# One fused attention and expert kernel on Trainium2: the chunk stage runs six tiles ahead instead of seven, with written lists for the prologue and for the last seven ticks

## The chip, the cores and the metric

One core of a Trainium2 chip. The metric is the device time of one execution in microseconds, the median of three runs. TensorE (PE in the profile) does matmuls and transposes; its weight loads are listed as PEld. VectorE (DVE), ScalarE (ACT) and GpSimd (POOL) work on tiles, and SyncE (SP) issues the transfers (DMA). Each engine works through its own queue in order and waits at the head of it for what an instruction needs. TensorE's clock has two levels, 1.2 and 2.4 GHz; the profile gives the granted clock as a share of the higher.

## The reference, cut to what matters

```
scores = scale * (q_c @ k_c^T)                # chunk attention: 64 rows, 8 heads, B = 8, S = 576
x = softmax(scores) @ v_c                     # 4608 rows x 512
logits = x @ w_gate                           # top 2 of 4 experts, softmax weights w
for e in range(4):
    a = softmax(causal(scale * (x @ wq[e]) @ (x @ wk[e])^T))
    out += mask_e * w_e * (a @ (x @ wv[e]) @ wo[e])
xn = layernorm(out) * g_ln
result = out + relu(xn @ w_ch1) @ w_ch2
```

## The kernel before, in words

The 4608 rows are 36 tiles of 128; nine tiles are a pair of batches, three tiles a group. A program of three kinds of work runs on them as a pipeline. The **chunk stage** of a tile takes q, k and v from memory: scores (`chunk_scores`, L145), shift by the row maximum (`chunk_shift`, L153, two VectorE instructions), exponential (`chunk_exp`, ScalarE), sum and reciprocal (`chunk_sum`, VectorE), scaling (`chunk_scale`, L171, GpSimd), turn (`chunk_turn`, L173: four transposes on TensorE and a copy on ScalarE), values (`chunk_values`, L181), and the split of the result x into a high part `xTh` (ScalarE) and the rest `xTl` (VectorE, `chunk_split`, L189), so that products keep more digits. The **projections** of a group (`proj_group`, L226) are seven pieces: four of `rows_` (k and q for two pairs of experts, 12 matmuls each) and three of `vals` (v and the gate's logits, one per tile). Each piece returns a copy for ScalarE and one for VectorE. The **attention** of a tile: scores (`attn_scores`, L328), masked shift (L376), exponential (L381), sums (`attn_sums`), weighing on GpSimd (`attn_weigh`, L398), transposes (`attn_turn`, L409), values (`attn_values`, L428), output projection (`attn_out`, L438) and the store to `xs`. A tile sees 1 to 5 key blocks of 128; at 5 it is "wide". When all is done, the second stage (normalising, two large matrix products, L838 and L1003) follows.

A **tick** s (`tick`, L557) does one step of each: the chunk stage of tile s, the chunk values of tile s-1, a few pieces of projections, and attention of tile g = s - `LA` (with transposes of g-1 and values and output of g-2). `LA` is 7: tiles 0 to 6 go through the chunk stage in a prologue. The order inside a tick is a string in `PLAN`, one letter per step, taken from left to right: S0 and S1 the scores of two pairs of experts, D0, D1, E0, E1 their masked shifts and exponentials, C chunk scores and values, H and X the split into xTh and xTl, N, n, R, r the chunk's shift, exponential, sum, scale, K and k its turn, O, Z, z attention values, Y, y output projection, L, W sums and weighing, T transposes, P or Q a piece of projections with a and v its two copies, G1 to G3 the gate, B one step of the conversion of the next stage's weights, F0, F1 (`fill`) one step of the preparation of the next stage. Four lists serve all ticks: by whether the tick is the third of a group, and wide.

The ticks 7 to 36 stand in a `manual_schedule`, in which TensorE, VectorE, ScalarE and GpSimd keep the order of the program. The prologue ahead of them and the ticks 37 to 44 don't: there a scheduler sets the order of each engine. SP's order is the scheduler's throughout.

The prologue's string `PRO` (L640) names loads of tiles (L), filler matmuls on zeros (`warm`, w), scores up to scale of a tile (S, five steps in one), turn with copy (P), values with split (X), a piece of the first group's projections with its copies (Q), and K, the next weights from `load_w` (L125). `load_w` loads a half of a weight into `wraw`, of which there are two buffers, and splits it into high (ScalarE) and low (VectorE) parts: wk, wq, wv, then wo, in this order. `pc`, the chunk probabilities, has two buffers as well.

## Time and profile before

| what | value |
|---|---|
| median of 3 runs | 1208.11 us (1207.94 to 1209.19) |
| the profiled execution | 1207.34 us, its span 1205.6 us |
| TensorE busy | 1179.7 us (98%) |
| VectorE, ScalarE, GpSimd busy | 902.2, 584.3, 266.6 us (75%, 48%, 22%) |
| mean granted clock of TensorE | 0.994 |

The span runs from the first to the last instruction; the execution's own time is 1.7 us longer. The attention of tile 0 begins at 49.28 us, and the second stage's first matmul at 466.03 us. TensorE is the engine that is nearly always busy, so that time is lost where it waits, runs at the lower clock, or does what the result doesn't need.

### The profile page before, as it was taken

The numbers are of one execution on the slowest core, as the hardware profiler recorded it, in microseconds if no ns is written. First come the engines' busy times: TensorE is split into PE (matmuls) and PEld (weight loads), VectorE is DVE, ScalarE is ACT, GpSimd is POOL, SyncE is SP. The second block draws the span as 40 slices with busy tenths as digits, with TensorE's granted clock in tenths as the row PEclk, the third lists the DMA queues.
The fourth block names the chain that finished last, engine by engine and source line by source line (L and its number), as shares of the span: only waits on it lengthen the run. The fifth ranks groups of instructions, "written<-read, shape, count | busy, mean of one in ns | idle before, by whom it ended". The sixth has DMA issues, their size and how long they took to land.

```text
span 1205.6 us, 29187 instructions
## 1 busy us (share of the span) xinstructions
PE 1179.7 (98%) x11874; PEld 1128.3 (94%) x11874; DVE 902.2 (75%) x1837; ACT 584.3 (48%) x1117; POOL 266.6 (22%) x480
## 2 busy tenths in 40 slices
PE   7989999999999999999999999999999999999998
PEld 5879998999999888999999999999999999999998
DVE  5688888888888768866865776556998777877782
ACT  3466566666566776533433343345454334333340
POOL 2245444644555331211121211110000000000000
PEclk8989999999999999999999999999999999999999
DMA  8333443434332236665455554658865445444521
GB/s 278 103 118 131 145 141 129 141 125 148 120 122 74 80 123 219 204 202 184 151 173 180 166 187 164 188 155 268 282 230 184 157 155 162 158 158 161 172 80 44
DMA packets 95845, 191.69 MB, mean 159 GB/s; under 512 B 8544, under 2 KB 42336, under 8 KB 94816
## 3 DMA queue, kind: packets, MB, share of 16 engines
q1 hardware_dynamic: 95712, 189.83, 47.4%
q8 instruction: 93, 1.52, 0.5%
q14 instruction: 40, 0.33, 0.1%
HBM read 118.50 MB, written 71.30 MB: 157 GB/s over the span
## 4 chain that ended last, share of the span: by engine, by line
PE 88%; DVE 6%; DMA 2%; ACT 1%; POOL 1%; issue 1%; SPq 0%; DVEq 0%; POOLq 0%; ACTq 0%
PE bb L838 17%; PE bb L1003 16%; PE ad L838 13%; PE ad L1003 12%; PE pp L246 7%; PE pv L273 4%; PE y_ps L438 4%; PE oa_ps L428 4%; PE tp L409 3%; PE sp L358 3%; PE tp L729 2%; PE sx_ps L151 1%; PE pT_ps L177 1%; DVE P L376 1%; PE sx_ps L187 1%
## 5 line engine op out<-in xcount | busy, mean ns | idle before, releaser
L838 PE MATMUL bb<-x,w1u 128*128 128x256 f32 x1728 | 216.6, 281 | 0.0
L838 PEld LDWEIGHTS bb<-x,w1u 128*128 128x128 f32 x1728 | 209.6, 188 | 0.3 <-ACT p L859 0.2
L838 PE MATMUL ad<-x,w1u 128*128 128x256 f32 x1296 | 173.3, 283 | 0.0
L838 PEld LDWEIGHTS ad<-x,w1u 128*128 128x128 f32 x1296 | 160.5, 188 | 0.2 <-issue 0.2
L1003 PE MATMUL bb<-w2u,hn 128*128 128x256 f32 x640 | 120.5, 280 | 1.5 <-DVE hn L951 1.5
L1003 PE MATMUL bb<-w2u,hx 128*128 128x256 f32 x584 | 109.5, 281 | 0.9 <-DVE xr L1014 0.9
L381 ACT ACTIVATE P<-P,nm 128x128 f32<-128x128 f32 (+8 forms) x144 | 87.2, 608 | 44.4 <-DVE nm L376 37.0
L398 POOL TENSOR_SCALAR P<-P,l 128x128 f32<-128x128 f32 (+8 forms) x144 | 94.5, 673 | 39.8 <-DVE l L391 24.8
L1003 PEld LDWEIGHTS bb<-w2u,hn 128*128 128x128 f32 x640 | 97.2, 189 | 1.7 <-DVE hn L951 1.7
L1003 PEld LDWEIGHTS bb<-w2u,hx 128*128 128x128 f32 x584 | 89.1, 189 | 1.0 <-PE bb L1003 1.0
L1003 PE MATMUL ad<-w2u,hn 128*128 128x256 f32 x440 | 80.7, 281 | 0.0
L1003 PE MATMUL ad<-w2u,hx 128*128 128x256 f32 x432 | 78.7, 281 | 0.0
L484 POOL TENSOR_TENSOR cv<-cv 128x512 f32<-128x512 f32 x16 | 25.5, 1594 | 235.8 <-DVE cv L480 218.3
L514 POOL TENSOR_TENSOR cw<-cw 128x128 f32<-128x128 f32 x128 | 62.3, 505 | 54.6 <-issue 46.4
L171 POOL TENSOR_TENSOR pc<-pc,lc 128x512 f32<-128x512 f32 x36 | 37.8, 1051 | 140.7 <-DVE lc L167 83.3
L1003 PEld LDWEIGHTS ad<-w2u,hn 128*128 128x128 f32 x440 | 65.7, 189 | 0.0
L1003 PEld LDWEIGHTS ad<-w2u,hx 128*128 128x128 f32 x432 | 64.9, 189 | 0.0
L376 DVE CUSTOM_DVE_ANT_0 P<-sp,mcaus 128x128 f32<-128x128 f32 (+7 forms) x128 | 59.9, 517 | 3.7 <-PE sp L358 3.6
L428 PE MATMUL oa_ps<-pTa,vg 128*64 128x128 f32 x928 | 59.4, 277 | 0.3 <-DVE pTa L413 0.3
L747 DVE TENSOR_TENSOR x<-xt,x 128x512 fp32r<-128x512 f32 x63 | 45.0, 722 | 19.2 <-ACT x L746 19.2
L409 PE MATMUL tp<-ident,P 128*128 128x128 f32 x464 | 57.9, 274 | 1.4 <-POOL P L398 1.3
L409 PEld LDWEIGHTS tp<-ident,P 128*128 128x128 f32 x464 | 52.0, 141 | 4.8 <-POOL P L398 1.8
(356 smaller groups left out, 2826.5 us busy)
## 6 DMA issues: line engine op xcount, KB each, us to landing
qk<-in_qk SPq DMA_DIRECT2D x36, 512.0 KB, 4.3
raw<-in_w_ch SPq DMA_DIRECT2D x32, 512.0 KB, 3.7
hx<-hd SPq DMA_DIRECT2D x28, 512.0 KB, 4.2
hn<-hd SPq DMA_DIRECT2D x25, 512.0 KB, 4.1
vb<-in_v SPq DMA_DIRECT2D x36, 256.0 KB, 4.4
xs<-y SPq DMA_DIRECT2D x36, 256.0 KB, 2.1
xc<-xs SPq DMA_DIRECT2D x18, 512.0 KB, 4.4
hd<-p SPq DMA_DIRECT2D x36, 256.0 KB, 4.0
```

Of the source, the lines that this page charges most:

```text
L246: nc.tensor.matmul(pp, a[:, f, ws], b_[:, f, :], start=(f == 0 and n == 0), stop=(f == KF - 1 and n == 2))
L273: nc.tensor.matmul(pv, a[:, f, cs], b_[:, f, :], start=(f == 0 and n == 0), stop=(f == KF - 1 and n == 2))
L376: nc.vector.tensor_tensor_reduce(dst, src, mk, -1.0, -3.0 * NEG, OP.add, OP.min, nm[:, e2:e2 + 1])
L381: nc.scalar.activation(pe, pe, AF.Exp, bias=nm[:, e2:e2 + 1], scale=-1.0, accum_out=l[:, e2:e2 + 1])
L398: nc.gpsimd.tensor_scalar(pe, pe, sums_[g][:, ep, e2:e2 + 1], 1.0, OP.mult, OP.mult)
L409: nc.tensor.transpose(tp[:, i, :], P[ep][e2][:, kt * 128:(kt + 1) * 128], ident)
L428: nc.tensor.matmul(o_ps[e2 * HD:(e2 + 1) * HD, ep, :], vg[:, gk % GT, e * HD:(e + 1) * HD], pT[:, e * n + kt, :], start=(kt == 0), stop=(k ...
L438: nc.tensor.matmul(y_ps, a[:, e2, :], b_[:, e2, :], start=(e2 == 0 and i == 0), stop=(e2 == EP - 1 and i == 2))
L514: nc.gpsimd.tensor_tensor(w[:, o, :], w[:, x, :], w[:, y, :], op)
L747: nc.vector.tensor_tensor(t[:, 1], tsum[i], f32(t[:, 0]), OP.subtract)
L838: nc.tensor.matmul(out[:, p], w[:, kt, a, WI[i], :], x[:, b_, kt, :], start=(start and p == 0 and kt == 0 and q == 0), stop=False, skip_gr ...
L1003: ins = nc.tensor.matmul(to[:, t], x[:, c, ts], w2u[i][:, w, half * 4 + c, :], start=start, stop=False, skip_group_check=True)
```

## The change

`LA` becomes 6, so that the prologue takes tiles 0 to 5 through the chunk stage and there is one more tick with chunk work; a group's projections begin in the tick in which the values of its last chunk tile are computed, after its X. The prologue becomes one written list inside the manual schedule, in which each load (c), high part (h), low part (l on VectorE, p on GpSimd) of a half weight, each chunk step and each piece of the first group's projections (P, a, v) has its place; `wraw` has six buffers; fillers go from 90 to 54. Ticks in the middle get five lists, by the tick's place in the group (s modulo 3) and wide or not; ticks 37 to 43 get a list each, and ticks 37 to 41 are scheduled by hand as well. `F` takes a step of the preparation wherever it stands, and a list may hold up to six. The number of steps B per tick stays seven.

```diff
-    def split(hi, lo, src, sc=None):
...
+    PARTS = [c + h for c in "kqvo" for h in "01"]
+
+    def weight_load(n):
+        src = part_of(n)[2]
+        raw = se.tile([128, 2 * VW], F32, name="wraw", bufs=6)[:, :src.size() // 128]
+        if n[0] != "o":
+            raw = raw.rearrange("p (a b) -> p a b", a=2)
+        nc.sync.dma_start(raw, src)
+        raws[n] = raw
...
+    paired = {}
+
     def early_scores(g):
-        acc = pair_tile(pss, "s_ps", "ps2")[:, :, :HP, :]
-        chunk_scores(g, acc)
-        chunk_shift(g, acc)
-        chunk_exp(g)
-        chunk_sum(g)
-        chunk_scale(g)
+        paired[g] = pair_tile(pss, "s_ps", "ps2")[:, :, :HP, :]
+        chunk_scores(g, paired[g])
 
     def early_values(g):
         acc = pair_tile(pss, "x_ps", "ps2")[:, :, :HP, :]
         chunk_values(g, acc)
-        for f in chunk_split(g, acc):
-            f()
+        paired[g] = list(chunk_split(g, acc))
...
     PLAN = {
-        "": "S0 S1 C D0 E0 D1 H G2 N O B Z X E1 n z R r P a v B T B G3 F0 L B Y P y a W B F1 B v K k B",
-        "3": "S0 D0 S1 E0 C H G2 D1 N E1 O X Z P G3 z n R r B a v Q a v L W B F0 T Y B y P a v B G1 B B K k F1 B",
-        "w": "S0 D0 C E0 O P Z N z n H X R r F0 S1 a D1 v E1 L B L1 Y y T B P B W B B a v W1 K B F1 B k",
-        "3w": "S0 C D0 H N E0 O Z X n P R z Q a v r a v S1 L D1 T B Y B F0 W B y E1 B P a v L1 G1 K B W1 k B B F1",
+        "p1": "S0 S1 D0 B C N E0 H O P D1 Z B z X n R a E1 v B T Y r L B P y a W v K B k B B",
+        "p1w": "S0 D0 C E0 O Z N S1 n P z H R D1 r X E1 a L Y W v y L1 B B T B B P a v B K W1 B k B",
+        "p2": "S0 D0 S1 C O E0 H D1 Z E1 N B P n a z X B R v Q a B v r L B W T Y B y P K a B B v G1 k",
+        "p2w": "S0 C H N D0 O X Z n R P E0 Q a z v r a v B B S1 Y D1 B K y L B E1 L1 T W W1 P B a v k G1 B B",
+        "p0": "S0 S1 D0 D1 C H E0 G2 N n E1 X G3 R O Z L z T P a v B r B W B Y B P y a K B v k B B",
+        "37": "S0 F D0 O S1 F D1 E0 Z P L z E1 a L1 F v W T P a v W1 Y F F y",
+        "38": "O S0 S1 Q D0 D1 Z z F E1 a E0 P v F a L v F F F Y y T P a W v G1 F",
+        "39": "G2 S0 D0 O G3 S1 D1 E0 Z F z F T P E1 a F P F L F W a v v Y y",
+        "40": "O S0 S1 D0 D1 Z P a z F E0 F T v F E1 Y L P W y F a v F",
+        "41": "P S0 O D0 Q F Z E0 a S1 v a z F D1 v F L T F F W P Y y E1 F a v L1 W1 G1",
+        "42": "O T Z z Y y F",
+        "43": "O Z T z F Y y",
     }
...
-        if s >= GT + 1 and (s - GT - 1) % GT == 0 and (s - GT - 1) // GT < NT // GT:
-            projs.append(proj_group((s - GT - 1) // GT))
-        three = (s - GT - 1) % GT == 2
+        three = s % GT == 2
...
         def proj(big=False):
+            if s % GT == 0 and not projs and 1 < s // GT <= NT // GT:
+                projs.append(proj_group(s // GT - 1))
...
-        for op in PLAN[("3" if three else "") + ("w" if wd else "")].split():
-            if op in do:
+        for op in PLAN[str(s) if str(s) in PLAN else f"p{s % GT}" + ("w" if wd else "")].split():
+            if op[1:] in PARTS:
+                start_up(op)
+            elif do.get(op):
                 do[op]()
...
-    LA = 7
+    LA = 6
     MID = NT + 1
-    TAIL = NT + 4
+    TAIL = NT + 3
...
-    PRO = ("L0 L1 L2 K w22 T0 w12 S0 w12 T1 L3 K S1 w12 P0 T2 "
-           "L4 K S2 P1 X0 w20 T3 L5 K S3 X1 w12 P2 T4 L6 S4 "
-           "X2 P3 Q X3 Q L7 T5 S5 P4 Q T6 X4 L8 S6 P5 Q "
-           "Q Q X5 P6 Q ")
...
+    PRO = ("w40 L0 c0 L1 L2 ck1 ck0 L3 N0 n0 c1 N1 w14 n1 R0 r0 R1 cq0 c2 cq1 K0 k0 N2 r1 n2 R2 hk0 V0 hk1 r2 K1 k1 V1 "
+           "H0 H1 K2 pk0 pk1 k2 V2 X1 c3 hq0 X0 H2 X2 L4 P cv0 hq1 lq1 N3 n3 a cv1 lq0 R3 r3 hv1 P v K3 hv0 c4 a v k3 V3 "
+           "L5 H3 N4 n4 pv1 c5 P a co0 X3 R4 r4 lv0 P K4 v k4 a N5 v V4 H4 P co1 n5 L6 R5 a r5 P P ho0 v a ho1 a X4 K5 v "
+           "lo0 v k5 L7 po1 G")
...
+    with tc.manual_schedule(engines=ALL):
+        for op in PRO.split():
+            start_up(op)
+        bg(LA)
...
-    for s in range(MID, TAIL):
-        tick(s, fill)
+    with tc.manual_schedule(engines=ALL):
+        for s in range(MID, TAIL):
+            tick(s, fill)
...
-    for s in range(TAIL, NT + LA):
-        tick(s, fill)
+    with tc.manual_schedule(engines=ALL):
+        for s in range(TAIL, NT + LA):
+            tick(s, fill)
```

Three places show how rows move. First, TensorE in the prologue, where the chunk tiles 2 and 3 meet the first projection (s_ps are chunk scores, pT_ps turns, x_ps chunk values, pp a row projection, wkh and wkl the parts of wk, wp fillers; the numbers keep the buffers of the tiles apart). Before:

```order
L97 LDWEIGHTS wz_161
L97 MATMUL wp_474<-wz_161 128x256
L177 MATMUL pT_ps_487<-ident_123,pc_359 128x128 x4
L151 MATMUL s_ps_498<-qk_328 64x64 x16
L187 MATMUL x_ps_525<-pTc_492,vb_182 64x64 x16
L177 MATMUL pT_ps_544<-ident_123,pc_447 128x128 x4
L246 MATMUL pp_559<-xTl_392,wkh_165 128x384
```

After:

```order
L163 MATMUL s_ps_306<-qk_241 64x64 x16
L189 MATMUL pT_ps_325<-ident_123,pc_255 128x128 x4
L199 MATMUL x_ps_343<-pTc_330,vb_217 64x64 x16
L189 MATMUL pT_ps_364<-ident_123,pc_277 128x128 x4
L199 MATMUL x_ps_371<-pTc_369,vb_238 64x64 x16
L189 MATMUL pT_ps_390<-ident_123,pc_334 128x128 x4
L199 MATMUL x_ps_399<-pTc_395,vb_242 64x64 x16
L163 MATMUL s_ps_417<-qk_249 64x64 x16
L255 MATMUL pp_450<-xTl_361,wkh_165 128x384
```

Before, the turn of tile 2 is followed by tile 4's scores, then come the values of tile 2, the turn of tile 3 and the projection; the fillers ahead of it are the last of 90. After, the first row is the scores of tile 2, and the turns and values of tiles 0, 1 and 2 follow without a filler; the scores of tile 3 stand directly ahead of the first projection, those of tile 4 behind it.

Second, TensorE in the middle, in the tick that attends tile 12 (four key blocks; sp are attention scores, sx_ps the chunk stage, oa_ps attention values, tp transposes). Before:

```order
L358 MATMUL sp<-kWh,qh 128x512 x2
L151 MATMUL sx_ps<-qk 64x64 x16
L187 MATMUL sx_ps<-pTc,vb 64x64 x16
L428 MATMUL oa_ps<-pTa,vg 64x128 x8
L246 MATMUL pp<-xTl,wkh 128x384
L246 MATMUL pp<-xTh,wkl 128x384
L246 MATMUL pp<-xTh,wkh 128x384
```

After:

```order
L367 MATMUL sp<-kWh,qh 128x512 x2
L163 MATMUL sx_ps<-qk 64x64 x16
L199 MATMUL sx_ps<-pTc,vb 64x64 x16
L437 MATMUL oa_ps<-pTa,vg 64x128 x8
L418 MATMUL tp<-ident,P 128x128 x12
L255 MATMUL pp<-xTl,wkh 128x384
L255 MATMUL pp<-xTh,wkl 128x384
L255 MATMUL pp<-xTh,wkh 128x384
```

The twelve transposes, which stood behind the twelve matmuls of this projection, now stand in front of them.

Third, VectorE in the second tick (tile 1 of the attention; P<-sp is the masked shift, nmc and pc the chunk's shift, xTl its low part). Before:

```order
L376 ISA P,nm<-sp,mcaus 128x256
L376 ISA nm 128x1
L376 ISA P,nm<-sp,mcaus 128x256
L376 ISA nm 128x1
L155 TENSOR_REDUCE nmc<-sx_ps 128x8
L157 TENSOR_TENSOR pc<-sx_ps,nmc 128x2x4x64
L196 TENSOR_TENSOR xTl<-sx_ps,xTh 128x4x128
```

After:

```order
L385 ISA P,nm<-sp,mcaus 128x256
L385 ISA nm 128x1
L385 ISA P,nm<-sp,mcaus 128x256
L385 ISA nm 128x1
L167 TENSOR_REDUCE nmc<-sx_ps 128x8
L169 TENSOR_TENSOR pc<-sx_ps,nmc 128x2x4x64
L385 ISA P,nm<-sp,mcaus 128x256
L385 ISA nm 128x1
L385 ISA P,nm<-sp,mcaus 128x256
L385 ISA nm 128x1
L208 TENSOR_TENSOR xTl<-sx_ps,xTh 128x4x128
```

The chunk's shift has moved ahead of the last two masked shifts.

## Rows read from the trace of the kernel before

**Rows 1.** Busy time of each engine, granted clock (PEclk) and DMA by stretch.

```profile
0.00:50.00 50.00, 40.32 (x630) 34.08 (x630) 27.29 (x57) 20.27 (x36) 11.19 (x23) 0.93 0.62 212
50.00:80.00 30.00, 25.71 (x338) 23.32 (x337) 24.88 (x77) 16.25 (x47) 12.41 (x20) 0.89 0.30 98
80.00:400.00 320.00, 318.88 (x4178) 289.19 (x4178) 269.32 (x769) 202.40 (x509) 162.78 (x305) 1.00 0.37 126
400.00:470.00 70.00, 65.47 (x581) 55.91 (x582) 55.34 (x161) 52.54 (x115) 23.86 (x54) 1.00 0.33 116
```

**Rows 2.** The chain of waits in the first 50 us: start, length, what.

```profile
4.88 7.43 DMA wraw<-in_wk
...
19.63 4.21 DMA wraw<-in_wv
...
25.27 2.83 DMA wraw<-in_wo
...
30.14 2.38 PE pp L246 x12
...
37.27 0.70 DVE pc L157
38.00 0.64 ACT pc L161
38.66 0.70 DVE lc L165
...
39.96 1.05 POOL pc L171
41.06 0.66 PE pT_ps L177 x4
...
43.16 2.11 PE pp L246 x12
45.27 1.43 PE pv L273 x12
46.70 0.62 PE x_ps L187 x32
```

**Rows 3.** Groups of instructions from 0 to 50 us: the filler matmuls.

```profile
L97 PE MATMUL wp<-wz 128*128 128x256 bf16 x90 | 13.1, 312 | 1.1 <-DVE wz L90 1.1
```

**Rows 4.** Three stretches of one microsecond, columns as in the first group.

```profile
14.00:15.00 1.00, 0.00 (x0) 0.00 (x0) 1.00 (x4) 0.00 (x0) 0.38 (x1) 0.61 0.88 306
20.00:21.00 1.00, 1.00 (x7) 0.69 (x6) 0.97 (x4) 0.30 (x1) 0.30 (x1) 0.50 0.74 234
26.00:27.00 1.00, 0.35 (x22) 0.35 (x26) 1.00 (x3) 0.59 (x2) 0.00 (x0) 1.00 0.69 234
```

**Rows 5.** Timeline of TensorE: chunk scores of tile 1, first scores of attention tiles 0 and 3.

```profile
8.36 0.69 PE L151 MATMUL s_ps<-qk 64*64 64x64 f32 x32
...
49.28 0.33 PE L358 MATMUL sp<-kWh,ql 64*128 64x128 f32 x2
...
80.56 0.49 PE L358 MATMUL sp<-kWh,ql 64*128 64x512 f32 x2
```

**Rows 6.** Whom TensorE waited for between 50 and 80 us: total, times, longest.

```profile
PE pT_ps L177 <- DVE l L389: 3.4, 1, 3.4
```

**Rows 7.** Timeline of the tick that attends tile 12, TensorE and VectorE.

```profile
186.67 0.50 PE L358 MATMUL sp<-kWh,ql 64*128 64x512 f32 x2
...
188.25 0.69 PE L151 MATMUL sx_ps<-qk 64*64 64x64 f32 x32
...
190.19 0.68 DVE L376 CUSTOM_DVE_ANT_0 P<-sp,mcaus 128x512 f32<-128x512 f32 x1
...
190.37 0.44 PE L246 MATMUL pp<-xTl,wkh 128*128 128x384 f32 x1
...
192.58 1.47 PE L409 MATMUL tp<-ident,P 128*128 128x128 f32 x12
...
193.74 0.68 DVE L196 TENSOR_TENSOR xTl<-sx_ps,xTh 128x512 fp32r<-128x512 f32 x1
```

More of the change, by code (lines that the diff above doesn't have):

```diff
@@ L125, in load_w @@
[L125 to L138 removed]
+            nc.scalar.activation(hi, raws[n], AF.Copy)
+        else:
+            nc.scalar.activation(hi, raws[n], AF.Copy, scale=sc)
@@ L558, in tick @@
         g = s - LA
-        if s + 2 < NT:
+        if s + 2 < NT and s + 2 not in loaded:
             load_tile(s + 2)
-        if s >= GT + 1 and (s - GT - 1) % GT == 0 and (s - GT - 1) // GT < NT // GT:
-            projs.append(proj_group((s - GT - 1) // GT))
         live, wd = 0 <= g < NT, 0 <= g < NT and wide(g)
-        three = (s - GT - 1) % GT == 2
+        three = s % GT == 2
         do, highs, lows = {}, [], []
@@ L654, in tile_kernel @@
                 projs.append(proj_group(0))
-            for f in next(projs[0]):
-                f()
-        elif c == "P":
-            chunk_turn(n)()
-        elif c != "T":
-            {"S": early_scores, "X": early_values}[c](n)
-    next(projs.pop(0))
-    step(gates[0])
-    bg(LA)
-    E_ = mybir.EngineType
-    with tc.manual_schedule(engines={E_.PE, E_.DVE, E_.Activation, E_.Pool}):
+            high, low = next(projs[0])
+            highs.append(high)
+            lows.append(low)
+        elif c == "a":
+            highs.pop(0)()
+        elif c == "v":
+            lows.pop(0)()
+        elif c == "G":
+            next(projs.pop(0))
+            step(gates[0])
+        elif c == "N":
+            chunk_shift(int(n), paired.pop(int(n)))
+        elif c == "K":
+            paired[n, "k"] = chunk_turn(int(n))
+        elif c == "k":
+            paired.pop((n, "k"))()
+        elif c in "HX":
+            paired[int(n)].pop(0)()
+        else:
+            prologue[c](int(n))
```

64 lines of the change are left out of this document (33 added, 31 removed).

## The prediction

> **What bounds the kernel now.** I read the stages first. TensorE is busy for 318.9 of the 320 us between 80 and 400 us, but only for 40.3 of the first 50, 25.7 of the next 30 and 65.5 of the 70 between 400 and 470 [rows 1]. So the middle is bound by TensorE and cannot gain from an order; 9.7 + 4.3 + 4.5 us of idle time lie where the change works. In the first 50 us the busy time also holds 13.1 us of 90 filler matmuls that compute nothing [rows 3].
>
> The chain of waits says why the first projection starts only at 30.14 us: it runs through the weights. The load of wk (7.43 us), that of wv (4.21) and that of wo (2.83) stand in it one after the other, each behind the splits of the one before [rows 2]: `wraw` has two buffers, so wv can be asked for only when wq has been split, and wo only when wv has. wo is not needed before the first output projection, yet its split stands in front of the split of tile 2's x on VectorE.
>
> Then the clock. It was granted at its lower level (0.50, 1.2 GHz) at 20 to 21 us, after it had fallen in the microsecond from 14 (0.61), in which TensorE did nothing; at 26 to 27 us, with TensorE busy for 0.35 us, it was 1.00 [rows 4]. In the first three ticks (50 to 80 us) the mean grant is 0.89 [rows 1]: some 30 x 0.11 = 3.3 us of work lost, after the turn of a chunk tile had waited 3.4 us, the longest of the waits there [rows 6].
>
> **The prologue.** The change removes 36 of 90 fillers, gives `wraw` six buffers, moves wv and wo behind the projections that don't need them, and takes one chunk tile (scores, turn, values) out. I walk its order with durations of the trace. Loads come in the same order up to wk, so tile 1's scores start at 8.36 us as now, when their load lands [rows 5], and are ready at 9.05; tile 0 has six more fillers ahead of it (0.15 us each by [rows 3]), and VectorE, by my estimate, is done with its shift at 9.3. From there a tile costs two instructions of 0.70 us for the shift, 0.64 for the exponential, 1.1 for the sum (0.70 and two small instructions), 1.05 for the scale on GpSimd, 0.66 for the turn and 0.62 for the values [rows 2], and some 0.6 for the copy, an instruction of the exponential's size. Tile 1's shift ends at 10.7, tile 0's sum at 11.8, its scale at 12.9, its turn at 13.6. The second half of tile 2's shift needs that turn's buffer of `pc` (two there are): 14.3; exponential 14.95; sum 16.1; scale 17.2; turn, behind tile 1's values, 18.0; copy 18.7; values 19.4; xTh (as the copy) 20.1; xTl 20.9; ten handings-over at some 0.05 us: the first projection at 21.4 instead of 30.14. The splits of wk now lie on ScalarE between exponentials and, for the low half, on GpSimd behind the last scale: 17.2 + 2 x 1.05 = 19.3, hidden with 2 us to spare; if GpSimd needed half as much again it would still be hidden, since only the eighth matmul wants the second half.
>
> From there to the first tick TensorE has four row projections at 2.1 to 2.4 us and three value projections at 1.44 [rows 2], 13.2 us; three turns, two scores and two values, 4.3 us; and waits that I count from the order of VectorE and ScalarE: 0.4 for the first half of wq's low part, 0.4 for wv's, 0.8 for tile 4's turned copy. The first tick starts at 21.4 + 19.1 = 40.5 us instead of 49.28 [rows 5]: 8.8 us, of which I take 8.7. The chunk tile taken out is done later, in a tick that TensorE bounds: scores, turn and values at 0.6 each, 1.8 us. **Net 6.9 us.** The ends: nothing of 1.6 us of waits (8.5), or a chain slower by 0.3 us at each of ten steps (3.9).
>
> **The first three ticks** last 31.3 us now, from 49.28 to 80.56 [rows 5]: 4.3 us idle and 3.3 lost to the clock, so 23.7 of work. The first one's new list puts the projection right behind the chunk stage. VectorE does four masked shifts (0.2 us each by my estimate, a quarter of the columns for which [rows 7] shows 0.68), the gate, tile 6's shift (1.4) and then tile 5's xTl (0.65), from 0.4 us into the tick: 3.7 us, while TensorE is there after 1.9: a wait of 1.8 us. In the second the new list issues the chunk's shift ahead of two of the masked shifts: exponential, sum and scale come 0.7 us earlier, and the tick starts with less conversion work ahead of them on VectorE; I find the scaled tile 0.95 us after TensorE wants it, instead of 3.4. A wait this short has not lowered the clock in the trace, so the third tick is free of it. With 0.5 us for what I don't see the three take 23.7 + 1.8 + 0.95 + 0.5 = 27.0 us against 31.3, a gain of 4.3; I take **4.2 us**; bounds 0 (the 3.4 us wait and the low clock stay) and 7.6 (all waits and the clock).
>
> **The middle.** Here nothing can be gained but the waits of 1.1 us, and there is a new one. With one tile less ahead, the first projection of a group reads the x of a tile whose values are computed in the same tick. Its matmul is queued on TensorE behind scores, chunk, values and (moved ahead of it) the transposes; behind it lie the output projection, the second projection and the turn, which feed VectorE, ScalarE and the next tick. At four key blocks the tick now has xTl from 193.74 to 194.42 us, 7.75 us after its first score matmul [rows 7]; but VectorE did parts of a conversion first. In the new list only the four masked shifts (0.68 us each), gate, shift and xTl stand there: some 5.7 us. TensorE arrives after scores 1.58, chunk 1.1, values 1.03 and transposes 1.47 [rows 7], at 5.2: a wait of 0.5. At three key blocks I take 0.4, at one none. Ten such ticks after the first: **-1.5 us** net, between +1 and -24 (the slower rival below).
>
> **The last seven ticks.** 4.5 us of idle time lie there [rows 1]. The lists written for them spread the preparation of the next stage (normalising, operand splits, first weight splits) from tick 37 on, five or six pieces a tick instead of two, so that ScalarE and VectorE have less of it at the end; but all engines now keep the written order, and in tick 39 ScalarE has a table load, two weight splits and an operand ahead of the exponentials that the next transposes need. I take a third of the idle time: **+1.5 us**, between -3 and +4.5.
>
> **Sum.** 6.9 + 4.2 - 1.5 + 1.5 = 11.1 us. The profiled execution took 1207.34 us (1205.6 of span and 1.7 around it): 1196.2. The median of the runs, 1208.11, lies 0.8 above it: **1197.0 us**.
>
> **Rivals.** *The low clock comes back.* Between 13 and 21 us the new order leaves TensorE idle half the time, with gaps up to 1.4 us and no fillers. For it: the clock fell at 14 us in the trace. Against: before that TensorE had stood still for over three microseconds, and at 26 us it kept the full clock at a third busy [rows 4]. If it falls, the turns and values on the path, or the first projections, run at half speed for the 6.6 us that this spell lasted: 3.3 us, 1200.3; with a later spell in the ticks, 1203. The Trainium skill (TensorE: Matmul & The Clock Gate, section "Part 1: The HAM clock gate") says that the slow level is the default and that only activity releases it, which speaks against taking fillers away; the trace agrees that idleness lowers the clock, and no row shows it at this density.
>
> *The waits of the early ticks stay.* VectorE is busy for 24.9 of 30 us there [rows 1]; if the scale of tile 7 comes as late as now, 3.4 us are waited, the clock falls, and the 4.2 us are gone: 1201.
>
> *Slower: the projection waits for xTl in every third tick.* If VectorE's lag stays as it is now, xTl ends 7.75 us into the tick and TensorE, there at 5.2, waits 2.5 us; over eleven ticks 28 us against the 1.5 + 1.8 already in the sum, that is 1197 + 24 = 1221. Against it: the conversion steps now stand behind xTl in the list. It turns the sign from (11.1 + 3.3) / 11 = 1.3 us a tick on.
>
> *Better:* the prologue without waits and most of the tail's idle time: 6.9 + 1.6 + 4.2 + 4 = 16.7, less 0.5: 1192.
>
> **Chances.** The forecast (1193 to 1200) 0.57; low clock or a slipping chain 0.16; early waits 0.10; better (1188 to 1193) 0.10; slower 0.05; no change, where several terms cancel, 0.02, with another 0.02 from the tails of the second and third. A difference under 0.2% (2.4 us) can't be told from none. Faster 0.91, same 0.04, slower 0.05. The range from 1190 to 1204 takes in the low clock and the early waits.
>
> **What would show it.** In the new profile: first projection at 21 to 22 us and first tick at 40 to 41; no load of wv or wo in the chain of waits; grant 1.00 from 12 to 70 us; the turn's wait in the second tick under 1.5 us; a wait of projections on xTl of about 1.8 us once and 0.5 after; TensorE's idle time between the last ticks about 3 us. Wrong it would be by a grant of 0.5 after 12 us, by waits on xTl over 1 us in each third tick, or by a tail whose transposes wait for GpSimd for longer than now.

## The result and the profile after

The changed kernel takes 1220.03 us (median of 4 runs, 1219.03 to 1221.33) against 1208.03 us (4 runs): the ratio is 1.0102, with an interval from 1.0089 to 1.0114. It is slower by 12 us, where a gain of 11 was forecast. The profiled execution has a span of 1217.3 us against 1205.6. The second stage's first matmul comes at 478.7 us instead of 466.0, so all of the loss lies ahead of it; behind it 1.0 us are won back.

The stages of the kernel after, with the columns of [rows 1]:

```profile
0.00:50.00 50.00, 39.10 (x596) 34.06 (x597) 28.34 (x72) 21.35 (x44) 17.15 (x32) 0.91 0.62 212
50.00:80.00 30.00, 27.59 (x377) 24.87 (x376) 26.54 (x76) 17.57 (x47) 14.91 (x26) 0.98 0.35 122
80.00:400.00 320.00, 310.65 (x4066) 280.47 (x4065) 267.24 (x741) 196.86 (x497) 154.52 (x290) 1.00 0.37 123
400.00:470.00 70.00, 60.82 (x541) 51.62 (x541) 56.70 (x179) 48.15 (x108) 23.26 (x57) 0.95 0.29 100
```

Compared with [rows 1], the stretch from 50 to 80 us is better (27.59 us busy instead of 25.71, clock 0.98 instead of 0.89), though it leaves out most of the first tick, which now begins at 43.23. But between 80 and 400 us TensorE, which hardly ever waited there, is now idle for 9.35 us, and between 400 and 470 us for 9.18 instead of 4.53, with a clock of 0.95.

Cutting the trace at the first score matmul of each tile shows where the account of the prediction breaks. The numbers are differences of such starts; tile 29 is the last with chunk work in the kernel after.

| stretch | before | after | difference | forecast |
|---|---|---|---|---|
| to the first tick | 49.28 | 43.23 | -6.05 | -8.7 |
| tiles 0 to 2 | 31.28 | 29.68 | -1.60 | -4.2 |
| tiles 3 to 28 | 307.79 | 319.76 | +11.97 | +1.5 |
| tile 29 (one more chunk tile) | 9.93 | 10.83 | +0.90 | +1.8 |
| tile 30 to the second stage | 67.75 | 75.18 | +7.43 | -1.5 |
| second stage to the end | 739.6 | 738.6 | -1.0 | 0 |

**The middle.** Whom TensorE waited for in the kernel after, from 72 to 400 us (total, times, longest). Here pp is a row projection, y_ps the output projection and tp a transpose; zl is the low part of the attention values, kWl that of the projected keys, xTl that of x, and den the sum in the gate's last step:

```profile
PE pp L255 <- DVE den L317: 4.4, 3, 1.7
PE y_ps L447 <- DVE zl L440: 4.3, 8, 1.5
PE tp L418 <- DVE den L317: 1.2, 2, 0.8
```

The loss sits in the nine ticks p0, in which the projections of a group begin (tiles 3, 6, ... 27); they take 119.79 us in sum instead of 107.23; the others are at most 0.3 us longer, some 0.2 shorter. The longest is the tick of tile 12, which took 12.39 us before and now 15.31. Here are TensorE (PE), VectorE (DVE) and GpSimd (POOL) in it:

```profile
181.59 0.50 PE L367 MATMUL sp<-kWh,ql 64*128 64x512 f32 x2
...
182.22 0.95 DVE L489 SCALAR_TENSOR_TENSOR cvt<-raw,cvt 128x512 f32<-128x512 uint32 x1
...
184.04 0.68 DVE L385 CUSTOM_DVE_ANT_0 P<-sp,mcaus 128x512 f32<-128x512 f32 x1
...
185.48 1.79 PE L418 MATMUL tp<-ident,P 128*128 128x128 f32 x12
...
188.12 0.68 DVE L208 TENSOR_TENSOR xTl<-sx_ps,xTh 128x512 fp32r<-128x512 f32 x1
...
188.71 0.16 DVE L317 TENSOR_REDUCE den<-ex 128x3 f32<-128x12 f32 x1
...
188.94 0.41 PE L255 MATMUL pp<-xTl,wkh 128*128 128x384 f32 x1 [1.67 <-DVE den L317]
...
189.20 0.66 DVE L177 TENSOR_REDUCE lc<-pc 128x8 f32<-128x512 f32 x1
...
189.59 1.30 POOL L493 TENSOR_TENSOR cvt<-cva,cvt 128x512 f32<-128x512 f32 x1
...
189.89 1.03 DVE L178 TENSOR_SCALAR lc<-lc 128x8 f32<-128x8 f32 x1
...
191.33 1.04 POOL L183 TENSOR_TENSOR pc<-pc,lc 128x512 f32<-128x512 f32 x1 [0.44 <-PE pp L255]
...
191.51 0.88 DVE L400 TENSOR_TENSOR l<-l,wg 128x4 f32<-128x4 f32 x1
192.31 0.41 DVE L440 TENSOR_TENSOR zl<-oa_ps,zh 128x256 fp32r<-128x256 f32 x1
...
192.78 0.50 PE L447 MATMUL y_ps<-woh,zl 128*128 128x512 f32 x1 [1.49 <-DVE zl L440]
```

Two consumers wait. The first projection is ready at 187.27 us (188.94 less 1.67) and waits for xTl, which ends at 188.80, and the end that the profile names (den) stands right behind it in VectorE's order. The output projection is ready at 191.29 and waits for zl, which ends at 192.72: in the list p0 the letter z stands behind the gate's last step, the chunk's sum and the attention sums. VectorE comes to the first masked shift only at 184.04, 2.45 us into the tick, because a conversion step of the tick before (here its last instruction, at 182.22) and four small instructions (the copy of the gate's logits and the gate's first three) are still ahead of it. Before, it came to them later still, 2.92 us into the tick, but there no projection read an x of the same tick. Of the time ahead of zl, 1.6 us are two small instructions that took 1.03 and 0.88 us instead of 0.17 and 0.16 (see the last section).

**The tail.** The tick of tile 33 (list 39), 16.06 us long against 5.93 before:

```profile
444.41 1.09 PE L418 MATMUL tp<-ident,P 128*128 128x128 f32 x8
...
445.21 1.28 ACT L750 ACT_TABLE_LOAD   x1
...
446.70 1.77 ACT L727 ACTIVATE w1u<-w1u 128x896 fp32r<-128x896 f32 x2
...
447.73 1.92 DVE L758 TENSOR_SCALAR xc<-xc,mv,rs 128x512 f32<-128x512 f32 x4
448.38 0.61 ACT L783 ACTIVATE x<-xt 128x512 fp32r<-128x512 f32 x1
...
449.50 1.28 ACT L390 ACT_TABLE_LOAD   x1
449.56 2.09 DVE L728 TENSOR_TENSOR w1u<-w1u 128x896 fp32r<-128x896 f32 x2
...
451.56 0.42 DVE L440 TENSOR_TENSOR zl<-oa_ps,zh 128x256 fp32r<-128x256 f32 x1
...
452.13 0.76 PE L447 MATMUL y_ps<-woh,zl 128*128 128x512 f32 x1 [6.62 <-ACT P L390]
```

The output projection waits 6.62 us for zl, which ends at 451.98. Ahead of zl on VectorE stand four normalisations and two weight splits; these wait for ScalarE, which does a table load, the square roots, two high parts of weights and an operand, then a second table load, before the exponentials of the tile go on. In written order no engine can let attention's small instructions pass. The clock then falls as well, from 450.4 to 457.2 us: the tick's mean grant is 0.80.

**The prologue.** The first projection starts at 22.65 us (forecast 21.4). The fillers ahead of tile 0's scores, 34 before and 40 after:

```profile
1.12 5.26 PE L97 MATMUL wp<-wz 128*128 128x256 bf16 x34 [1.12 <-DVE wz L90]
```

```profile
1.13 7.22 PE L97 MATMUL wp<-wz 128*128 128x256 bf16 x40 [1.13 <-DVE wz L90]
```

The six more take 2.0 us instead of the 0.9 that the prediction gave them, and VectorE is done with tile 0's shift at 10.46 us instead of 9.3. Eight microseconds each from 12 and from 20 us, columns as in [rows 1]:

```profile
12.00:20.00 8.00, 3.29 (x76) 2.38 (x76) 5.16 (x13) 4.76 (x9) 4.42 (x5) 1.00 0.91 329
20.00:28.00 8.00, 7.26 (x83) 7.07 (x84) 5.39 (x10) 3.49 (x8) 2.23 (x3) 0.57 0.88 291
```

The clock, 1.00 up to 20 us with TensorE busy for 3.29 of the 8 us, fell at 20.3 us and came back at 27.1.

### The profile page after: what moved, and what is told of

Read it like the earlier page. It is cut to its first block, busy times and chain, and to the rows that moved or that the text cites. A ratio compares the mean times of both kernels' runs of the same rounds, so it can differ in the third digit from the quotient of the medians.

```text
span 1217.3 us, 29146 instructions
## 1 busy us (share of the span) xinstructions
PE 1179.1 (97%) x11838; PEld 1126.6 (93%) x11838; DVE 907.1 (75%) x1833; ACT 584.2 (48%) x1117; POOL 268.5 (22%) x484
## 4 chain that ended last, share of the span: by engine, by line
PE 81%; DVE 12%; ACT 3%; POOL 2%; issue 2%; DMA 0%; DVEq 0%; ACTq 0%; POOLq 0%
PE bb L877 17%; PE bb L1042 16%; PE ad L877 13%; PE ad L1042 12%; PE pp L255 6%; PE y_ps L447 3%; PE pv L282 3%; PE sp L367 3%; PE oa_ps L437 3%; PE tp L418 2%; PE tp L766 2%; DVE P L385 1%; DVE pc L169 1%; PE sx_ps L163 1%; POOL P L407 1%
```

## Experiments

The lengths below are cut from each trace at the first score matmul of tiles 0, 3, 29 and 30 and of the second stage. Times are medians; the ratio is to runs of the kernel before on the same chip. Each row of lengths is one trace.

| kernel | time | ratio, interval | to tile 0 | tiles 0-2 | tiles 3-28 | tile 30 to stage 2 |
|---|---|---|---|---|---|---|
| before | 1208.03 | | 49.28 | 31.28 | 307.79 | 67.8 |
| after | 1220.03 | 1.0102 (1.0089 to 1.0114) | 43.23 | 29.68 | 319.76 | 75.2 |
| x and z early in p0 | 1223.52 | 1.0133 (1.0117 to 1.0150) | 43.55 | 29.45 | 322.52 | 76.8 |
| seven ahead, new lists | 1224.41 | 1.0139 (1.0123 to 1.0154) | 48.09 | 29.28 | 321.19 | 73.9 |
| old end | 1211.02 | 1.0028 (1.0017 to 1.0039) | 43.22 | 29.66 | 319.58 | 66.2 |
| list 39 altered | 1224.25 | 1.0133 (1.0114 to 1.0152) | 44.40 | 30.87 | 319.58 | 78.1 |
| old end, old p0 list | 1226.17 | 1.0150 (1.0134 to 1.0165) | 44.31 | 31.25 | 330.60 | 68.7 |
| old end, z early | 1219.60 | 1.0099 (1.0082 to 1.0115) | 42.44 | 30.83 | 327.57 | 66.9 |
| before with new prologue | 1206.82 | 0.9993 (0.9984 to 1.0003) | 48.20 | 30.33 | 307.65 | 68.0 |
| tail lists, two F a tick | 1226.08 | 1.0151 (1.0136 to 1.0166) | 43.49 | 29.90 | 319.56 | 82.4 |
| mix | 1202.67 | 0.9952 (0.9939 to 0.9965) | 48.04 | 29.50 | 305.94 | 67.1 |
| mix with fillers | 1201.18 | 0.9939 (0.9926 to 0.9951) | 46.95 | 29.50 | 306.38 | 67.6 |
| tail lists, scheduled | 1213.93 | 1.0044 (1.0028 to 1.0060) | 42.59 | 30.81 | 319.48 | 68.3 |
| six ahead, list for VectorE | 1208.98 | 1.0011 (1.0001 to 1.0021) | 41.85 | 28.46 | 320.39 | 66.0 |
| old end, two B moved | 1214.17 | 1.0061 (1.0045 to 1.0078) | 43.92 | 32.60 | 319.74 | 66.2 |
| list for VectorE, two B moved | 1212.32 | 1.0042 (1.0027 to 1.0057) | 41.08 | 31.34 | 322.37 | 66.0 |

Two further kernels, with one run each, do the conversion behind the ticks; their times don't compare.

### x and z early in the list p0

```diff
-"p0": "S0 S1 D0 D1 C H E0 G2 N n E1 X G3 R O Z L z T P a v ..."
+"p0": "S0 S1 C D0 H X E0 D1 N E1 n G2 G3 O Z z R r L T P a v ..."
```

> The changed kernel with one list altered, that of the middle ticks in which a group's projections begin: the split of x (H, X) stands directly behind the chunk stage and the first masked shifts, ahead of the other shifts, and z ahead of the chunk's sum. Theory 'order': the ticks are long because xTl and zl stand too late in VectorE's queue. Then the ten such ticks from tile 3 on lose most of their 10.5 us of TensorE idle time, the first tick loses 2.9 us of waiting and its spell of low clock, and the time falls from 1220 to about 1208 to 1211. Rival 'lag': VectorE comes into these ticks late whatever the list says, because conversion steps of the tick before are still in its queue; then at least half of the waits stay and the time is above 1215. Rival 'displacement': the masked shifts are now late, transposes and weighing wait, and it stays at 1218 to 1222.

1223.5 us, slower than after. The waits changed their names, not their sum: the 4.4 us for the first projection's x are gone, but a later projection waits 5.8 us in eight places behind the copy of y, transposes 1.9 us for masked shifts, zl is still waited for with 1.8 (in this list the gate stood ahead of it again), kWl with 1.6. The middle is 2.8 us longer than after. 'Order' falls; 'displacement' is what the trace shows, with a time 1.5 us above its range. 'Lag' isn't excluded: what it asked for, half of the waits and a time above 1215, is met as well.

### Seven tiles ahead, all new lists kept

```diff
-    LA = 6
+    LA = 7
...
-... P P ho0 v a ho1 a X4 K5 v lo0 v k5 L7 po1 G"
+... c6 P P ho0 v a ho1 a X4 N6 K5 n6 v k5 R6 lo0 r6 v V5 H5 X5 L7 po1 L8 K6 k6 G"
```

> The changed kernel with the chunk stage seven tiles ahead again: tile 6 joins the prologue's list, and all lists of the ticks stay as they are, in the same phase. Theory 'one tile less ahead': the waits of the first projection (7.2 us in all) go, with the low clock of the first tick (1.6 us), while the waits of the output projection for zl (4.3 us in the middle) stay; the prologue is 2 to 3 us longer, and the last tick of chunk work 1.8 us shorter: about 1211 to 1213. Rival 'lists': the new lists are the cause and not the look-ahead; the same ticks stay 1 to 3 us longer than before and the time is 1217 or more. The tail keeps its 6.6 us wait in both.

1224.4 us: the rival 'lists'. Now no projection needs an x of its own tick, and the first projection waits for nothing; the middle is as long all the same (321.19; a spell of low clock behind the longest wait is part of it, a mean of 0.90 in the tick of tile 12). TensorE's waits from 77 to 398 us:

```profile
PE y_ps L447 <- DVE zl L440: 9.2, 8, 3.4
PE tp L418 <- DVE den L317: 1.1, 2, 0.8
```

The wait has moved one consumer down: TensorE comes earlier to the output projection, and zl stands as late in p0 as it did. So the list p0 alone, without the shorter look-ahead, costs as much.

### The end as before

```diff
-    with tc.manual_schedule(engines=ALL):
-        for s in range(MID, TAIL):
-            tick(s, fill)
+    for s in range(MID, TAIL):
+        tick(s, fill)
...
-        for op in PLAN[str(s) if str(s) in PLAN else f"p{s % GT}" + ("w" if wd else "")].split():
+        for op in PLAN[(f"p{s % GT}" if s < MID else "3" if three else "") + ("w" if wd else "")].split():
```

The ticks from 37 on take the four old lists, with two steps of preparation in each.

> The changed kernel with the end as it was: no written order on the engines after tick 36, the four general lists, two steps of preparation in a tick. Theory 'tail lists': the wait of 6.6 us in the tick of tile 33 and the low clock behind it come from the written lists; from the first score of tile 30 to the second stage 67 to 69 us instead of 75.2, and 1212 to 1214. Rival: the end is longer because one tile less ahead leaves more to do after the chunk work; then 1218 or more.

1211.0 us, 9.0 less than after, all of it behind tile 30 (66.2 instead of 75.2 us). The theory holds, and more than it asked: the end is 1.6 us shorter than before.

### Only list 39 altered

```diff
-"39": "G2 S0 D0 O G3 S1 D1 E0 Z F z F T P E1 a F P F L F W a v v Y y"
+"39": "G2 S0 D0 O G3 S1 D1 E0 Z z F T P E1 a Y y P L F W F a v v F F F"
```

> The changed kernel with only the list of tick 39 altered: z stands directly behind Z, y behind the transposes, and the weight splits and operands (F) at the end of the tick. Theory 'queue': the output projection waited 6.6 us for zl only because norm, two weight splits and a table load stood ahead of it; the wait and the low clock behind it go, and the time falls by 6 to 8.5 us to 1212 to 1214. Rival 'work': ScalarE and VectorE have that much to do in this tick in any case, and the wait moves to the next tick's scores or transposes; the time falls by under 3 us.

1224.3 us: worse, and the theory 'queue' falls. The tick of tile 33 is 3.8 us shorter (12.29 instead of 16.06), the next 4.9 longer (10.25 instead of 5.32): the pTa copy that the attention values need stands behind the same splits now, as the row of TensorE shows.

```profile
455.95 0.66 PE L437 MATMUL oa_ps<-pTa,vg 128*64 128x128 f32 x8 [2.84 <-DVE pTa L422]
```

### The old end and the old list p0, six ahead

```diff
-"p0": "S0 S1 D0 D1 C H E0 G2 N n E1 X G3 R O Z L z T P a v B r B W B Y B P y a K B v k B B"
+"p0": "S0 S1 C D0 E0 D1 H G2 N O B Z X E1 n z R r P a v B T B G3 L B Y P y a W B B v K k B"
```

> The kernel with the old end (the run before this one that gave 1211.0), and in it the list p0 replaced by the general list of the kernel before, without its two steps of preparation; the chunk stage stays six tiles ahead. Theory 'place of zl': the tick was long because chunk sums, gate and sums stood ahead of zl on VectorE, and the output projection behind the first projection waited for it; in the old list zl comes right behind xTl. Then the nine ticks from tile 3 to 27 lose most of the 12.6 us that they were longer than before, and the time is 1200 to 1204. Rival 'one tile less ahead': the first projection now waits for xTl in the ticks of four key blocks, 2 us or more in each, since the transposes no longer stand ahead of it; the time stays at 1207 or more.

1226.2 us, 15 us more than with the new p0 list. One line holds all of TensorE's waits between 75 and 406 us:

```profile
PE pp L255 <- DVE xTl L208: 18.8, 9, 3.4
```

With zl early and the transposes behind, the first projection meets the dependency that the shorter look-ahead has made in each of the nine ticks, 2.1 us in the mean and 3.4 at most. In four of the nine ticks the clock fell as well (mean 0.89). The rival holds: this list is 24.7 us slower in the middle with six ahead than with seven (the mix below, which has the same lists in all middle ticks).

### Only the letter z moved

```diff
-"p0": "... N n E1 X G3 R O Z L z T P a v ..."
+"p0": "... N n E1 X O Z z G3 R L T P a v ..."
```

> The kernel with the old end, and in the list p0 only the letter z moved: directly behind Z, ahead of the gate's last step, the chunk's sum and the attention sums. Theory 'place of zl': the 4.3 us for zl go, the 4.4 us for the first projection and 1.2 of the transposes stay; 1204 to 1208. Rival 'VectorE is full': the tick of four key blocks has 12 us of VectorE work for 11.6 of TensorE, so that what is moved ahead of zl only delays the sums and the wait comes back elsewhere; 1210 or more.

1219.6 us, 8.6 more than without the move. The waits from 72 to 400 us:

```profile
PE pp L255 <- DVE kWl L273: 5.2, 3, 2.0
PE pp L255 <- ACT y L452: 4.4, 6, 0.7
PE pp L255 <- DVE xTl L208: 4.3, 3, 1.7
PE tp L418 <- DVE xTl L208: 1.1, 2, 0.8
PE pv L282 <- DVE kWl L273: 0.6, 1, 0.6
PE y_ps L447 <- DVE zl L440: 0.2, 1, 0.2
```

Those for zl are down to 0.2 us; the copies of the projections (kWl) and of y are late instead. The rival 'VectorE is full' holds.

### The kernel before with the new prologue alone

The edit: the kernel before with the prologue's list for seven tiles that is shown above, in written order; lists, ticks and end stay as they were.

> The kernel before with the new prologue alone (with tile 6 in its list, seven tiles ahead, the four old lists, the old end). The same prologue took 48.1 us to the first tick in the run with seven tiles ahead, against 49.3 before, with a spell of low clock in the first tick. Theory: it is worth 1 to 3 us there and the first ticks lose their wait for the turn: 1203 to 1206. Rival: the low clock takes it all back: 1207 to 1209.

1206.8 us, between the two ranges, and no difference that can be told (0.9984 to 1.0003); 2.0 us are won by tile 3 (78.53 instead of 80.56). Of 16 us from 12 on the granted clock was 0.64 and 0.51 in the halves, and 0.65 in the first tick. In the middle (307.65 us) TensorE waits for 0.9 us in all. With the runs above this closes a square: seven ahead with the old list p0, 307.7 (305.9 in the mix below, which shares the other lists with the rest); seven with the new, 321.2; six with the new, 319.6; six with the old, 330.6 us.

### The tail's lists with two steps of preparation

```diff
-"39": "... Z F z F T P E1 a F P F L F W a v v Y y"
+"39": "... Z F z F T P E1 a P L W a v v Y y"
```

In the other lists likewise the third and later F are left out.

> The changed kernel with its written lists for the last seven ticks, but at most two steps of preparation (F) in each, as before; the rest comes after the last tick. Theory 'preparation too early': ScalarE and VectorE are full in ticks 38 to 40 because five or six steps stand in each; with two, the end from tile 30 on takes 67 to 70 us instead of 75.2 and the time is 1212 to 1215. Rival 'written order': the engines in written order wait wherever one of them is late; the wait of the output projection in the tick of tile 33 stays at 3 us or more and the time is above 1216.

1226.1 us, and the end is 82.4 us long: 'too early' falls, 'written order' holds. The wait stands in the same tick:

```profile
440.27 1.09 PE L418 MATMUL tp<-ident,P 128*128 128x128 f32 x8
440.30 1.28 ACT L750 ACT_TABLE_LOAD   x1
...
441.21 0.69 DVE L743 BATCH_NORM_STATS2 st<-xc 128x6 f32<-128x512 f32 x1
...
443.84 0.66 DVE L743 BATCH_NORM_STATS2 st<-xc 128x6 f32<-128x512 f32 x1
...
444.83 0.42 DVE L440 TENSOR_TENSOR zl<-oa_ps,zh 128x256 fp32r<-128x256 f32 x1
...
445.30 0.79 PE L447 MATMUL y_ps<-woh,zl 128*128 128x512 f32 x1 [3.94 <-DVE zl L440]
```

zl (444.83) now has four statistics of the norm ahead of it instead of splits, and what is left out comes after the last tick.

### The mix, and the mix with fillers

```diff
-    LA = 6
+    LA = 7
...
-"p0": "S0 S1 D0 D1 C H E0 G2 N n E1 X G3 R O Z L z T P a v ..."
+"p0": "S0 S1 C D0 E0 D1 H G2 N O B Z X E1 n z R r P a v ..."
...
-... cq1 K0 k0 N2 ... k1 V1 ... k2 V2 ... V4 ... V5 ... K6 ...
+... cq1 w10 K0 k0 w4 N2 ... k1 w4 V1 ... k2 w4 V2 ... w4 V4 ... w6 V5 ... w10 K6 ...
```

Both have the prologue for seven tiles, the end as before and the new lists p1, p1w, p2 and p2w; only the second has the last line.

> A mix of both kernels: the new prologue with tile 6 in it, seven tiles ahead, the new lists p1, p1w, p2 and p2w for two of three ticks, the old general list for the ticks in which a group's projections begin, and the old end. Theory 'look-ahead and p0 list': the middle ticks cost nothing more than before, the new lists p1 and p2 save 0.1 to 0.2 us in a third of the ticks and 1.4 us of waiting in the second tick: 1203 to 1206. Rival: with the new lists around it the old p0 list waits again; 1208 or more.

> The mix with 42 filler matmuls put back into the idle gaps of the prologue, each batch shorter than its gap (10, 4, 4, 4, 4, 6 and 10, ahead of turns and values). Theory 'clock': the clock stays at its higher level from 14 to 28 us and in the first tick, where without them it was 0.50 to 0.61 for about 13 and 7 us; half of that is given back, 5 to 8 us less than the mix. Rival: fillers run late and push the turns back, or the clock falls all the same: within 2 us of the mix.

1202.7 and 1201.2 us, the fastest of all: the second beats the kernel before by 0.61% (0.49 to 0.74). The theory of the mix holds, 0.3 us under its range; its middle is 1.9 us shorter than before. The fillers held the clock at 1.00 up to the third tick (the first takes 7.84 us instead of 9.53); there it fell (mean 0.86), behind a wait of 2.5 us for a turn in the second. Of the 2.6 us won up to that tick 1.5 are lost in it; the medians lie 1.5 us apart with intervals that overlap, less than expected and within the rival's 2 us. The theory 'clock' is shown for the prologue and the first two ticks, not for the time.

### The tail's lists, order left to the scheduler

```diff
-    with tc.manual_schedule(engines=ALL):
-        for s in range(MID, TAIL):
-            tick(s, fill)
+    for s in range(MID, TAIL):
+        tick(s, fill)
```

Likewise for the ticks from `TAIL` on; the seven lists stay.

> The changed kernel with its seven lists for the last ticks, five or six steps of preparation in a tick as they are, but without the written order on the engines there: the scheduler sets it, as before. Theory 'written order': the wait of 6.6 us goes because attention's steps can overtake table loads and weight splits: 1209 to 1213, like the run with the old end. Rival 'preparation too early': it stays above 1216.

1213.9 us, 0.9 above the range of the theory that it bears out. The end is 68.3 us: of the 9.0 us that the new end costs, 6.9 come from the written order (the wait and the low clock behind it; here the clock stays at 1.00). The other 2.1 are within what the old end itself varies (66.0 to 68.7 us in six traces), so that a cost of the five or six steps isn't shown.

### Six ahead with a list written for VectorE

```diff
-"p0": "S0 S1 D0 D1 C H E0 G2 N n E1 X G3 R O Z L z T P a v B r B W B Y B P y a K B v k B B"
+"p0": "S0 S1 C D0 E0 D1 H X E1 O N Z z n T G2 P R r a v B Y G3 B L W B P y a B K v B k B B"
```

With the old end, and w10, w4, w4 and w4 in the gaps of the prologue.

> Six tiles ahead with the old end and 22 fillers in the prologue, and a list p0 written anew for VectorE: masked shifts, then xTl, the chunk's shift, zl, and only then gate, chunk sum and attention sums; on TensorE the transposes ahead of the first projection as in the changed kernel. Theory 'one tile less ahead binds whatever the list': at four key blocks VectorE has the conversion of the tick before, four shifts and xTl to do before TensorE's 5.2 us are over, so that 1 to 2 us of waiting stay in three ticks and 0.5 in others, and the nine ticks are still 5 us or more longer than before: 1202 to 1208. Rival 'only the list': the nine ticks are within 2 us of before, and with the shorter prologue the kernel falls under 1200.

1209.0 us. The prologue with fillers keeps the clock, as these rows show beside those of after:

```profile
12.00:20.00 8.00, 5.65 (x98) 4.18 (x96) 5.15 (x12) 4.76 (x9) 4.24 (x4) 1.00 0.90 321
20.00:28.00 8.00, 6.44 (x93) 5.57 (x92) 5.57 (x12) 4.48 (x9) 2.92 (x4) 1.00 0.88 292
```

It reaches the first tick at 41.85 us and tile 3 at 70.31, the earliest so far. In the ticks p0 half of the surplus is gone (112.82 us in sum against 107.23 before and 119.53 with the old end), and xTl and zl are waited for with under 1 us in all. But the middle takes 320.39 us: projections wait 3.6 us for kWl, scores 1.9 for a masked shift, value projections 1.7, much of it in the ticks behind. 'Binds whatever the list' holds for the lists that were tried, 1.0 us above its range.

### Two conversion steps moved out of p2

```diff
-"p1": "... a W v K B k B B"          "p2": "... y P K a B B v G1 k"
+"p1": "... a W v K B B B k B B"      "p2": "... y P K a v G1 k"
```

p1w and p2w alike; first with the list p0 of the change, then with the one for VectorE and the fillers.

> The kernel with the old end, six tiles ahead and the list p0 as it is; only two of the seven conversion steps (B) at the end of the lists p2 and p2w go to the end of the lists p1 and p1w. The sum over a group stays 21. Theory 'load carried over': in the tick of tile 12 VectorE begins its masked shifts up to 2 us earlier, the first projection and the output projection wait less, and the nine ticks p0 fall from 12.6 us over before to 5 or less: 1202 to 1206. Rival 'order alone': zl and xTl stand where they stand in the list, VectorE makes up nothing by starting earlier; the middle stays within 2 us of 319.6 and the time at 1209 or more. Rival 'moved only': the extra steps at the end of p1 make the p2 ticks longer by as much.

> The same move of two conversion steps in the kernel with six tiles ahead, the list p0 written for VectorE and 22 fillers in the prologue (1209.0 without the move). Theory 'load carried over': the middle falls from 320.4 to 310 to 314 us, and with the earliest tile 3 of all runs (70.3 us) the time is 1198 to 1203. Rival: the waits only move on, to kWl and masked shifts, and the middle stays at 318 or more.

1214.2 and 1212.3 us, both 3 us slower than without the move; the middle is 319.7 and 322.4 us. In the tick of tile 12 the first masked shift comes 2.06 us into the tick instead of 2.40: VectorE was behind all the same, and the p2 tick of tile 2 is 2.7 us longer (13.55 instead of 10.81), nearly the whole loss. In the middle of the first the ticks p0 gain 1.2 us and the ticks p2 lose 1.4. 'Moved only' holds; what 'order alone' asked for is met as well, and whether load or order is the cause stays open here.

### No conversion in the ticks

```diff
-        do["B"] = lambda: bg(s)
+        do["B"] = None
...
-            bg(s, 16)
+            bg(s, 16 + 7 * 31)
```

With the old end; first with the list p0 of the change, then with the old one.

> Six tiles ahead, old end, the list p0 as it is, and no conversion step (B) in any tick from 6 to 36: all 217 of them run in one block at the end of tick 36, so that only the lengths of the ticks count and not the time. That takes some 3 us of VectorE's work out of a tick and a little from ScalarE and GpSimd. Theory 'load': VectorE is level with TensorE, the nine ticks p0 are within 3 us in sum of those of the kernel before, and the waits for xTl, zl and kWl there are under 2 us. Rival 'order': the chain of dependent steps in p0 (gate and sums ahead of zl) is the cause and not the load; at least 7 us of the 12.6 stay.

> The same with the old list in p0, whose first projection waited 18.8 us for xTl in nine ticks. Theory 'load': without the conversion the wait falls to under 6 us. Rival 'dependency': xTl stands behind four masked shifts and the chunk's shift in any case, and TensorE is there after its 4 us of scores, chunk work and values; 12 us or more of the wait stay.

VectorE is busy for 204 and 197 of the 300 us from 80 on. The nine ticks p0 take 113.61 us with the new list (6.4 more than before; 12.3 more with conversion) and 119.63 with the old (12.4 more; 23.6 with conversion). Waits from 70 to 385 us, first new, then old:

```profile
PE y_ps L447 <- DVE zl L440: 2.9, 6, 0.6
PE pp L255 <- DVE den L317: 2.4, 3, 0.8
```

```profile
PE pp L255 <- DVE xTl L208: 12.3, 9, 2.3
```

The tick of tile 12 with the new list, which began at 181.65 us:

```profile
186.85 0.68 DVE L208 TENSOR_TENSOR xTl<-sx_ps,xTh 128x512 fp32r<-128x512 f32 x1
...
187.68 0.42 PE L255 MATMUL pp<-xTl,wkh 128*128 128x384 f32 x1 [0.80 <-DVE den L317]
```

With nothing carried over, xTl ends 5.88 us into the tick instead of 7.21, and the wait is 0.80 us instead of 1.67. Half of each surplus goes with the load, half stays. With the old list the waits themselves fall by a third only (18.8 to 12.3 us); the rest of the gain is mostly clock, which is now low in one of the nine ticks instead of four. 'Load' asked for under 3 us and falls short, 'order' for 7 and just misses; 'dependency' has its 12. But what stays for zl need not be order alone: ahead of it three small instructions took 5.9 us longer in the nine ticks than alone (0.17 us each), as the last section tells, and the waits for zl are 2.9 us.

## Why the prediction was wrong

**The prologue** was right in kind and short by a third. Chain and waits are close: no load of wv or wo in the chain of waits, the first projection at 22.65 instead of 21.4 us. Two steps failed. The estimate that VectorE is done with tile 0's shift at 9.3 us was 1.2 us too early, because the six more fillers took 2.0 us; in the run with 22 fillers in the gaps the first projection is as late (22.49). The other is the low clock, which stood as a rival with "no row shows it at this density": the clock was low from 20.3 to 27.1 us, through the whole first projection. From its start to the first tick it took 20.6 us, against 19.4 with those fillers and a clock of 1.00 (forecast 19.1).

**The early ticks.** The second has a wait of 1.0 us (forecast 0.95) and the third none (10.81 us at full clock), as argued. The first waits 2.9 us for xTl instead of 1.8, and that wait takes the clock with it (mean 0.84): 1.6 instead of 4.2 us.

**The middle** is the first large failure. The mechanism was seen (the first projection waits for an x of its own tick) and put at 0.4 to 0.5 us in the ticks p0, with a rival at 2.5. In the tick of tile 12, which was worked out, xTl ends 7.21 us into the tick, not 5.7, and the wait is 1.67 us, not 0.5: "only the four masked shifts, gate, shift and xTl stand there" left out that conversion steps queued at the end of the list before are carried over. Without conversion it ends at 5.88 us. The term was also added up too low: four ticks at 0.5 and three at 0.4 us are 3.2, less the 1.1 us of old waits 2.1, not 1.5. And it asked for xTl alone. The next consumer, the output projection, waits for zl, which the list had put behind gate and sums; its wait (4.3 us in the middle) is as large as that for xTl (4.4) and is in no term of the sum. In this place of the list the sums' small instructions run beside GpSimd's scaling and lose 6.9 us in the nine ticks, in each tick at least what zl is waited for, but for 0.1 us. So the place of zl costs by what stands ahead of it and by how long that is blocked; no run parts the two. The nine ticks cost 12.6 us, 1.4 each: the turning point of the slower rival was 1.3. (That nothing but 1.1 us of waits can be gained in the middle was also too little: the mix is 1.9 us shorter there.)

What the runs put in place of the forecast: seven ahead, the projections of a tick p0 ask for no x of that tick, so that TensorE first waits for VectorE's work of the tick at the output projection, and VectorE may fall behind in it and catch up in the next (11.8 us of work in the tick of tile 12, for 11.6 of TensorE's; TensorE waited 0.8 us there). Six ahead ends this. With the old list the first projection waits for xTl, 23.6 us longer in nine ticks; the new list puts the transposes ahead and zl last, 12.3 to 12.6 us longer, and 14.0 even where seven ahead makes it needless (121.20 us). Half of either goes when VectorE has no conversion to do; the other half stays with the dependent steps inside the tick and, for zl, with what is blocked ahead of it. That no list makes six ahead as cheap as seven is not shown: five were tried.

**The tail** is the second: +7.4 instead of -1.5 us. That in list 39 a table load, splits and an operand stand ahead of the exponentials was written down, and then a third of the idle time was taken as gain. The shown cause is the written order (6.9 us), not the number of steps: with two a tick in written order zl was still waited for with 3.94 us.

**The rivals.** The time of the slower one, 1221 us, came out by luck. Its mechanism, a wait of 2.5 us for xTl in every third tick, was seen in three ticks of nine and with 1.7 us at most. Of the 23 us between forecast and result 10.5 come from the middle, 8.9 from the tail and 5.3 from the prologue and the early ticks, less 1.9 elsewhere. Its chance of 0.05 was too low mainly because each of three weak spots was priced by one likely value, and the waits behind a wait by none.

## What to carry to other kernels

Where an engine of nearly the same load feeds the bound one, look-ahead is what lets it fall behind and catch up: count what its queue still holds from the step before, and ask for every consumer in the waiting engine's order, not only the first. Where preparation with waits of its own is mixed in, the scheduler's order was 6.9 us better here than the written one; whether a written order pays in the middle was not tested. Test the parts apart: the best parts with fillers are 18.9 us faster than all parts together.

## What the runs showed of the hardware

Two small VectorE instructions took as long as a GpSimd instruction that ran beside them: a TENSOR_SCALAR on 8 columns 1.03 us (189.89 to 190.92) while GpSimd's conversion ran to 190.89, and a product on 4 columns 0.88 us (to 192.39) while GpSimd scaled a chunk to 192.37; the same two took 0.17 and 0.16 us in the tick of tile 12 before, with GpSimd idle:

```profile
195.43 0.17 DVE L166 TENSOR_SCALAR lc<-lc 128x8 f32<-128x8 f32 x1
...
197.72 0.16 DVE L391 TENSOR_TENSOR l<-l,wg 128x4 f32<-128x4 f32 x1
```

The Trainium skill (SBUF — State Buffer, section "Who interferes with whom") says that the two engines share a port pair, held by one of them for its whole instruction while the other blocks; the rows agree. Not every small instruction is hit: up to 470 us of the trace after, that product took 0.72 us in the median of 20 times beside a GpSimd instruction and 0.16 in the median of 23 times without, but the reciprocal just ahead of it 0.17 to 0.18 us with or without. In the tick of tile 12 this puts 1.6 us ahead of zl, and 6.9 us in the nine ticks p0; in the kernel before nothing of it stands ahead of zl there.

The same prologue reached the first tick at 42.41 to 44.40 us in eleven traces, in which the clock fell at 13.8 to 20.3 us and stayed low for 6.8 to 13.7 us. With 22 fillers in its gaps the clock stayed at 1.00 in both traces that had them.
